# A decode layer with its gradients: key-value moments for dq, half of V kept on chip, 128-row weight layouts, and zero fills on a queue of their own

## Chip, cores and metric

One Trainium2 chip, one core. The time is device microseconds of one launch, from runs without and with the profiler; most agree within 0.3%. The kernel before takes 882.29 us (median of 5 runs, 880.35 to 884.32). All runs in this document are of the undisturbed ("fast") state, except where a single run has no state.

## The reference, cut to what matters

```
x: [1, 1, 448];  k_cache, v_cache: [1, 8, 32768, 256] bf16;  16 query heads, 8 key-value heads
W = 4096                                   # only the last 4096 rows of each cache are used
h   = x + attention(layernorm(x), k_cache[:, :, -W:], v_cache[:, :, -W:], wq, wo)
out = h + (g * u) @ w_down                 # g, u = layernorm(h) @ w_gate, @ w_up
returns out and the gradients of x, k_cache, v_cache, wq, wo, w_gate, w_up, w_down
```

The gradients of the two caches have the caches' shape. Of their 268.4 MB only the last 4096 rows of each head are not zero: 33.5 MB are computed, and 234.9 MB are written as zeros, in 112 fills of 2 MB. Each attention head pair (two query heads share one key-value head) needs K and V of 2.1 MB each.

## The kernel before

It runs in a first pass over the 8 head pairs (scores, softmax, output), a middle (output projection, gated layer, its backward, down to the gradient `do` of the attention output), and a second pass over the head pairs (dp = do V, ds, dq = ds K, and the two cache gradients as outer products). Nearly all transfers, the fills too, stand in one queue, SyncE's.

```python
    LD = nc.sync
    ST = nc.sync
    ...
    def issue_zero_fills(k):
        for _ in range(k):
            if zero_jobs:
                LD.dma_start(out=zero_jobs.pop(0), in_=zeros[:])       # zeros: [128, 8192] bf16
    ...
    wq_sb = wqp.tile([DC, NC, H * Dh], bf16, tag="wq")                  # DC, NC = 112, 4
    ...
    def load_kv_natural(pool, cache, g, tag, nb):
        t_ = pool.tile([128, T, Dh], bf16, tag=tag, bufs=nb)
        LD.dma_start(out=t_[:], in_=cache[0, g, Sk - W:, :].rearrange("(p t) d -> p t d", t=T))
        return t_
    ...
    LD.dma_start(out=wo_sb[:], in_=A_wo.rearrange("(jc p) n -> p jc n", p=128))   # rows of 896 bytes
    ...
    for g in range(G):                                   # first pass
        ...                                              # K^T by TensorE, scores, softmax -> pT_all[:, g]
        for t in range(T):
            nc.tensor.matmul(o_ps[:, :], lhsT=pT16[:, t, :], rhs=V_sb[:, t, :], ...)
        V_tiles[g + 1] = load_kv_natural(kv, A_v_cache, g + 1, "Vnat", 1)
    ...
    for it in range(G):                                  # second pass, g = 7 .. 0
        ...
        issue_zero_fills(Z2_LIST[it])
        if it >= 1 and g - 1 >= 0:
            V2[g - 1] = load_kv_natural(kv, A_v_cache, g - 1, "Vnat", 1)
            K2[g - 1] = load_kv_natural(kv, A_k_cache, g - 1, "Knat", 2)
        ...
        for t in range(T):                               # dq = ds K: K is needed again
            nc.tensor.matmul(dq_ps[:, :], lhsT=dsT16[:, t, :], rhs=K_sb[:, t, :], ...)
```

Of the kernel before, what the change touches and what calls it, by code (L numbers as in the profile page):

```python
# [7 lines left out]
bf16 = mybir.dt.bfloat16  # L8
# [6 lines left out]
DC = 112  # L15
NC = 4
H = 16
# [4 lines left out]
TH = 16  # L22
NR = T // TH
F = 1792
FC = 14
# [5 lines left out]
Z1, ZM, Z2, ZT = 6, 10, 6, 6  # L31
Z2_LIST = [6, 10, 6, 6, 6, 5, 5, 4]
# [3 lines left out]
def kernel(  # L36
        ctx, tc, A_x, A_k_cache, A_v_cache, A_wq, A_wo, B_x, B_w_gate, B_w_up, B_w_down, grad_out,
           out_0, out_1, out_2, out_3, out_4, out_5, out_6, out_7, out_8):
    nc = tc.nc

    const = ctx.enter_context(tc.tile_pool(name="const", bufs=1))
    small = ctx.enter_context(tc.tile_pool(name="small", bufs=2))
    lnp = ctx.enter_context(tc.tile_pool(name="lnp", bufs=1))
    psum_acc = ctx.enter_context(tc.tile_pool(name="psum_acc", bufs=1, space=bass.MemoryType.PSUM))
    psum_tr = ctx.enter_context(tc.tile_pool(name="psum_tr", bufs=2, space=bass.MemoryType.PSUM))
    psum_s = ctx.enter_context(tc.tile_pool(name="psum_s", bufs=1, space=bass.MemoryType.PSUM))
    psum = ctx.enter_context(tc.tile_pool(name="psum", bufs=2, space=bass.MemoryType.PSUM))
    psum_d = ctx.enter_context(tc.tile_pool(name="psum_d", bufs=2, space=bass.MemoryType.PSUM))

    LD = nc.sync  # L50
    ST = nc.sync
# [11 lines left out]
    zeros = const.tile([128, ZW], bf16)  # L63
    nc.vector.memset(zeros[:], 0.0)
    S_f = const.tile([H, 8, 128], f32)
    nc.gpsimd.memset(S_f[:], 0.0)
    nc.gpsimd.affine_select(out=S_f[:], in_=S_f[:], compare_op=ALU.not_equal, fill=1.0, base=0,
                            pattern=[[-1, 8], [1, 128]], channel_multiplier=-8)
    E_b = const.tile([2, 4], bf16)
    nc.gpsimd.memset(E_b[:], 0.0)  # L70
    nc.gpsimd.affine_select(out=E_b[:], in_=E_b[:], compare_op=ALU.not_equal, fill=1.0, base=-2,
                            pattern=[[1, 4]], channel_multiplier=-1)
# [7 lines left out]
    assert len(zero_jobs) == 8 * Z1 + ZM + 8 * Z2 + ZT  # L80

    def issue_zero_fills(k):
        for _ in range(k):
            if zero_jobs:
                LD.dma_start(out=zero_jobs.pop(0), in_=zeros[:])

    tc.swap_default_side()
    wq_pool = tc.tile_pool(name="wq_pool", bufs=1)
    wqp = wq_pool.__enter__()
    wq_sb = wqp.tile([DC, NC, H * Dh], bf16, tag="wq")  # L90
    tc.swap_default_side()
    for k in range(2):
        LD.dma_start(out=wq_sb[:, 2 * k:2 * k + 2, :], in_=A_wq.rearrange("(p c) j -> p c j", c=NC)[:, 2 * k:2 * k + 2, :])
    x_bf = lnp.tile([1, D], bf16, tag="ldrow_bf")
    LD.dma_start(out=x_bf[:], in_=A_x.rearrange("a b d -> (a b) d"))
    x_row = const.tile([1, D], f32)
    nc.vector.tensor_copy(out=x_row[:], in_=x_bf[:])
    go_bf = lnp.tile([1, D], bf16, tag="ldrow_bf")
    LD.dma_start(out=go_bf[:], in_=grad_out.rearrange("a b d -> (a b) d"))
    dh2_row = const.tile([1, D], f32)  # L100
    nc.vector.tensor_copy(out=dh2_row[:], in_=go_bf[:])

    def layernorm_row(xr, tagp):
        stats = lnp.tile([1, nc.vector.BN_STATS_DIM], f32, tag="stats")
        nc.vector.bn_stats(out=stats[:], in_=xr)
        mv = const.tile([1, nc.vector.BN_AGGR_DIM], f32, tag=tagp + "mv")
        nc.vector.bn_aggr(out=mv[:], in_=stats[:])
        rstd = const.tile([1, 1], f32, tag=tagp + "rstd")
        nc.scalar.activation(out=rstd[:], in_=mv[:, 1:2], func=ACT.Sqrt, bias=eps_t[0:1, 0:1], scale=1.0)
        nc.vector.reciprocal(out=rstd[:], in_=rstd[:])  # L110
        xn = const.tile([1, D], f32, tag=tagp + "xn")
        nc.vector.tensor_scalar(out=xn[:], in0=xr, scalar1=mv[:, 0:1], scalar2=rstd[:, 0:1], op0=ALU.subtract, op1=ALU.mult)
        xn_b = const.tile([1, D], bf16, tag=tagp + "xnb")
        nc.vector.tensor_copy(out=xn_b[:], in_=xn[:])
        xT_ps = psum.tile([DC, NC], f32, tag="tmp")
        for c in range(NC):
            nc.tensor.matmul(xT_ps[:, c:c + 1], lhsT=xn_b[0:1, c::NC], rhs=ones_bf[0:1, 0:1], start=True, stop=True)
        xT_b = const.tile([DC, NC], bf16, tag=tagp + "xTb")
        nc.vector.tensor_copy(out=xT_b[:], in_=xT_ps[:])
        xT_f = const.tile([DC, NC], f32, tag=tagp + "xTf")  # L120
        nc.vector.tensor_copy(out=xT_f[:], in_=xT_ps[:])
        return mv, rstd, xn, xn_b, xT_b, xT_f

    def ln_bwd_row(dy_ap, xhat, rstd, tagp):
        dy = lnp.tile([1, D], f32, tag="lnb_dy")
        if len(dy_ap.shape) == 3:
            nc.vector.tensor_copy(out=dy[:].rearrange("o (m c) -> o m c", c=dy_ap.shape[2]), in_=dy_ap)
        else:
            nc.vector.tensor_copy(out=dy[:], in_=dy_ap)
        s1 = lnp.tile([1, 1], f32, tag="lnb_s1")  # L130
        nc.vector.reduce_sum(out=s1[:], in_=dy[:], axis=AX)
        prod = lnp.tile([1, D], f32, tag="lnb_prod")
        s2 = lnp.tile([1, 1], f32, tag="lnb_s2")
        nc.vector.tensor_tensor_reduce(out=prod[:], in0=dy[:], in1=xhat, scale=1.0, scalar=0.0, op0=ALU.mult, op1=ALU.add, accum_out=s2[:])
        m12 = lnp.tile([1, 2], f32, tag="lnb_m12")
        nc.vector.tensor_scalar(out=m12[:, 0:1], in0=s1[:], scalar1=-1.0 / D, scalar2=None, op0=ALU.mult)
        nc.vector.tensor_scalar(out=m12[:, 1:2], in0=s2[:], scalar1=-1.0 / D, scalar2=None, op0=ALU.mult)
        t = lnp.tile([1, D], f32, tag="lnb_t")
        nc.vector.scalar_tensor_tensor(out=t[:], in0=xhat, scalar=m12[:, 1:2], in1=dy[:], op0=ALU.mult, op1=ALU.add)
        dx = lnp.tile([1, D], f32, tag="lnb_dx")  # L140
        nc.vector.tensor_scalar(out=dx[:], in0=t[:], scalar1=m12[:, 0:1], scalar2=rstd[:, 0:1], op0=ALU.add, op1=ALU.mult)
        return dx

    def bcast_row(row_ap, n, dst_bf):
        ps = psum.tile([128, n], f32, tag="tmp")
        nc.tensor.matmul(ps[:], lhsT=ones_f[0:1, 0:128], rhs=row_ap, start=True, stop=True)
        nc.scalar.copy(out=dst_bf, in_=ps[:])  # L147

    evac_ctr = [0]

    def evac_copy(out_ap, in_ap):
        if evac_ctr[0] % 2 == 0:
            nc.scalar.copy(out=out_ap, in_=in_ap)  # L153
        else:
            nc.vector.tensor_copy(out=out_ap, in_=in_ap)  # L155
        evac_ctr[0] += 1

    def load_kv_natural(pool, cache, g, tag, nb):
        t_ = pool.tile([128, T, Dh], bf16, tag=tag, bufs=nb)
        LD.dma_start(out=t_[:], in_=cache[0, g, Sk - W:, :].rearrange("(p t) d -> p t d", t=T))  # L160
        return t_

    def transpose_kv(X_sb, XT, evac=None):
        for q in range(8):
            tr_ps = psum_tr.tile([128, 4, 2, 128], bf16, tag="tr")
            for i in range(4):
                t = 4 * q + i
                for dh in range(2):
                    nc.tensor.transpose(tr_ps[:, i, dh, :], X_sb[:, t, dh * 128:(dh + 1) * 128], ident_bf[:])  # L169
            if evac is None:  # L170
                evac_copy(XT[:, 4 * q:4 * q + 4, :, :], tr_ps[:])
            else:
                evac(out=XT[:, 4 * q:4 * q + 4, :, :], in_=tr_ps[:])

    mv1, rstd1, xn_row, xn_bf, xnT_bf, xnT_f = layernorm_row(x_row[:], "ln1")
    qT_ps = psum.tile([128, 32], f32, tag="tmp")
    for col in range(32):
        for c in range(NC):
            nc.tensor.matmul(qT_ps[:, col:col + 1], lhsT=wq_sb[:, c, col * 128:(col + 1) * 128], rhs=xnT_bf[:, c:c + 1],  # L179
                             start=(c == 0), stop=(c == NC - 1))  # L180
    qT_bf = const.tile([128, 32], bf16)
    nc.vector.tensor_copy(out=qT_bf[:], in_=qT_ps[:])
    wq_pool.__exit__(None, None, None)

    kv_pool = tc.tile_pool(name="kv", bufs=2)
    kv = kv_pool.__enter__()
    work1_pool = tc.tile_pool(name="work1", bufs=2)
    work1 = work1_pool.__enter__()
    K_tiles = [None] * G
    V_tiles = [None] * G  # L190
    K_tiles[0] = load_kv_natural(kv, A_k_cache, 0, "Knat", 2)
    K_tiles[1] = load_kv_natural(kv, A_k_cache, 1, "Knat", 2)
    V_tiles[0] = load_kv_natural(kv, A_v_cache, 0, "Vnat", 1)

    tc.swap_default_side()
# [234 lines left out]
    with tc.tile_pool(name="work2", bufs=2) as work2, tc.tile_pool(name="rows", bufs=1) as rows, \  # L430
            tc.tile_pool(name="dkv", bufs=3) as dkv, tc.tile_pool(name="wgst", bufs=2) as wgst2:
        for it in range(G):
# [8 lines left out]
            for thunk in pending_stores:  # L441
                thunk()
# [140 lines left out]
```

## Time and profile before

| | before |
|---|---|
| time, median of 5 | 882.29 us |
| profiled span | 879.0 us |
| read / written | 76.65 / 280.59 MB |
| DMA queue's share of the 16 DMA engines | 98.8% |
| TensorE / VectorE / ScalarE busy | 47% / 31% / 22% |

The next fence has lines of the profile page of the kernel before. "DMA" is the mean busy share of the 16 DMA engines in 40 equal slices of the span, in tenths (9 is 90% or more); "GB/s" is what they moved.

```profile
span 879.0 us, 8996 instructions
...
PE 415.2 (47%) x3888; PEld 289.1 (33%) x3888; DVE 273.7 (31%) x554; ACT 189.7 (22%) x267; POOL 4.4 (0%) x14
...
DMA  9999999999999999999999999999999999999993
GB/s 289 364 334 428 429 430 426 429 422 431 424 423 428 431 424 426 429 418 429 430 428 430 426 418 429 428 429 429 420 430 429 417 402 424 401 423 354 432 368 122
...
q1 hardware_dynamic: 30180, 357.25, 98.8%
...
HBM read 76.65 MB, written 280.59 MB: 406 GB/s over the span
```

No engine that computes is busy for half of the span, and the DMA engines always are. This kernel is bound by its bytes. The rate is about 428 GB/s in most slices, and less at both ends. The table by stretches shows where. Its columns after the stretch and its length are busy time of TensorE, its weight loads, VectorE, ScalarE and GpSimd (with instruction counts), the granted TensorE clock, the DMA share, and GB/s.

```profile
5.00:10.00 5.00, 0.00 (x0) 0.00 (x0) 0.99 (x3) 0.00 (x0) 0.00 (x0) 1.00 1.00 269
10.00:15.00 5.00, 0.00 (x0) 0.00 (x0) 0.00 (x0) 0.00 (x0) 0.00 (x0) 1.00 0.97 269
...
45.00:50.00 5.00, 3.36 (x62) 2.51 (x59) 1.77 (x6) 0.48 (x4) 0.00 (x0) 1.00 1.04 269
50.00:55.00 5.00, 0.38 (x2) 0.30 (x2) 0.59 (x3) 0.16 (x2) 0.00 (x0) 0.58 1.01 247
...
100.00:200.00 100.00, 40.23 (x501) 31.20 (x500) 13.31 (x36) 14.09 (x24) 0.00 (x0) 0.65 1.01 427
...
800.00:820.00 20.00, 13.96 (x61) 8.91 (x61) 7.51 (x11) 6.28 (x12) 0.00 (x0) 0.53 1.01 365
...
850.00:860.00 10.00, 0.00 (x0) 0.00 (x0) 0.00 (x0) 0.00 (x0) 0.48 (x1) 0.50 0.97 276
860.00:870.00 10.00, 0.00 (x0) 0.00 (x0) 0.00 (x0) 0.00 (x0) 0.00 (x0) 0.50 0.48 161
870.00:879.00 9.00, 0.00 (x0) 0.00 (x0) 0.00 (x0) 0.00 (x0) 0.00 (x0) 0.50 0.09 39
```

From 5 to 15 us the DMA engines are full, yet move 269 GB/s: that is the load of wq in 112 rows. In the packet records of the trace its 16 KB packets take about 975 ns, where 16 KB packets elsewhere take 611 (16 engines times 16 KB in 611 ns are 429 GB/s). The stretch from 45 to 55 us has w_gate and w_up, also in 112 rows, and the first packets of w_down. After 850 us the last stores drain.

### The profile page before, as it was taken

To read this page: it belongs to the slowest core of one execution; us is meant where nothing else is said; L and a number is where in the kernel's file an instruction comes from. 1 tells how busy PE (TensorE), PEld (TensorE's weight loads), DVE (VectorE), ACT (ScalarE), POOL (GpSimd) and SP (SyncE) were. 2 spreads that over 40 slices of the span, in tenths; PEclk is the share of its full clock that TensorE was granted. 3 is DMA by queue.
4 is the path that set the end of the run, shared out by engine and by line. 5 is a ranking of instruction groups with operands and counts; after the bars stand their busy time and mean duration, and the time that the engine had idled before them with its cause. 6 is when DMAs were issued, how large, how long until landed. Compare 5 with 4: busy or idle time off the path is not lost.

```text
span 879.0 us, 8996 instructions
## 1 busy us (share of the span) xinstructions
PE 415.2 (47%) x3888; PEld 289.1 (33%) x3888; DVE 273.7 (31%) x554; ACT 189.7 (22%) x267; POOL 4.4 (0%) x14
## 2 busy tenths in 40 slices
PE   0824425060523208652199486382845748386400
PEld 0813314040413105441164153261623426163300
DVE  3311011020202000357963343432334434334760
ACT  0502011020202004051043132231323324233100
POOL 1000000000000000000000000000000000000000
PEclk9965667575757558655585556575655758575655
DMA  9999999999999999999999999999999999999993
GB/s 289 364 334 428 429 430 426 429 422 431 424 423 428 431 424 426 429 418 429 430 428 430 426 418 429 428 429 429 420 430 429 417 402 424 401 423 354 432 368 122
DMA packets 30283, 357.82 MB, mean 407 GB/s; under 512 B 3010, under 2 KB 7108, under 8 KB 9028
## 3 DMA queue, kind: packets, MB, share of 16 engines
q1 hardware_dynamic: 30180, 357.25, 98.8%
q8 instruction: 30, 0.49, 0.2%
q14 instruction: 9, 0.07, 0.0%
q0 software_dynamic: 64, 0.00, 0.0%
HBM read 76.65 MB, written 280.59 MB: 406 GB/s over the span
## 4 chain that ended last, share of the span: by engine, by line
issue 55%; DMA 31%; PE 8%; SPq 2%; DVE 1%; POOL 0%; ACT 0%; POOLq 0%
PE o_ps L264 5%; DMA t__537<-in_A_v_cache_dram 4%; DMA t__1393<-in_A_v_cache_dram 4%; DMA t__1607<-in_A_v_cache_dram 4%; DMA t__965<-in_A_v_cache_dram 4%; DMA t__1179<-in_A_v_cache_dram 4%; DMA t__751<-in_A_v_cache_dram 4%; DMA t__1819<-in_A_v_cache_dram 3%; DMA wd_sb<-in_B_w_down_dram 2%; DMA x_bf<-in_A_x_dram 2%; SPq L204 2%; PE ao_ps L306 1%; PE ffn_ps L327 1%; PE tr_ps L169 0%; PE qT_ps L179 0%
## 5 line engine op out<-in xcount | busy, mean ns | idle before, releaser
L155 DVE CAST stg<-d_ps 128x512 bf16<-128x512 f32 x128 | 88.2, 689 | 99.4 <-PE d_ps L496 75.5
L153 ACT CAST stg<-d_ps 128x512 bf16<-128x512 f32 x128 | 74.8, 584 | 176.5 <-DMA out_dram<-stg 92.4
L153 ACT COPY KT<-tr_ps 128x1024 bf16<-128x1024 bf16 x32 | 32.3, 1011 | 185.2 <-PE tr_ps L169 185.2
L153 ACT COPY VT<-tr_ps 128x1024 bf16<-128x1024 bf16 x28 | 28.4, 1012 | 54.5 <-PE tr_ps L169 28.6
L155 DVE COPY KT<-tr_ps 128x1024 bf16<-128x1024 bf16 x32 | 22.1, 691 | 47.8 <-PE tr_ps L169 47.7
L155 DVE COPY VT<-tr_ps 128x1024 bf16<-128x1024 bf16 x28 | 19.3, 690 | 31.3 <-PE tr_ps L169 29.7
L496 PE MATMUL d_ps<-R_sb,rows_3486 4*128 4x256 bf16 x64 | 16.2, 375 | 20.4 <-ACT stg L153 17.2
L496 PE MATMUL d_ps<-R_sb,rows_4256 4*128 4x256 bf16 x64 | 16.3, 378 | 19.9 <-ACT stg L153 17.0
L488 PE MATMUL r_ps<-ident_bf,pdsT 128*4 128x128 bf16 x256 | 21.0, 235 | 8.7 <-DVE pdsT L471 3.5
L496 PE MATMUL d_ps<-R_sb,rows_3877 4*128 4x256 bf16 x64 | 16.1, 371 | 18.2 <-ACT stg L153 15.2
L496 PE MATMUL d_ps<-R_sb,rows_3101 4*128 4x256 bf16 x64 | 17.1, 396 | 15.9 <-ACT stg L153 12.7
L496 PE MATMUL d_ps<-R_sb,rows_4633 4*128 4x256 bf16 x64 | 16.3, 377 | 15.2 <-ACT stg L153 12.3
L496 PE MATMUL d_ps<-R_sb,rows_5010 4*128 4x256 bf16 x64 | 15.4, 360 | 15.7 <-ACT stg L153 12.5
L374 DVE CUSTOM_DVE_ANT_0 junk<-wo_sb,dh_bc 128x448 bf16<-128x448 bf16 x32 | 20.0, 625 | 3.6 <-ACT dh_bc L147 2.6
L488 PEld LDWEIGHTS <-pdsT 128*4 128x4 bf16 x256 | 16.5, 90 | 11.9 <-issue 6.9
L286 DVE CAST o_bf<-o_ps 16x256 bf16<-16x256 f32 x1 | 0.4, 413 | 63.3 <-PE o_ps L264 63.3
L351 PE MATMUL bc_ps<-ident_f,dgu_f 128*128 128x128 f32 x56 | 13.1, 413 | 14.1 <-DVE dgu_f L342 10.2
L264 PE MATMUL o_ps<-t__1819,pT_1996 128*16 128x256 bf16 x32 | 5.4, 350 | 29.0 <-DMA t__1819<-in_A_v_cache_dram 29.0
L496 PE MATMUL d_ps<-R_sb,rows_5388 4*128 4x256 bf16 x64 | 15.7, 362 | 7.1 <-ACT stg L153 4.6
L353 ACT CAST dgu_bc<-bc_ps 128x512 bf16<-128x512 f32 (+1 forms) x8 | 15.9, 2296 | 12.8 <-PE bc_ps L351 12.8
L234 PE MATMUL sT_ps<-qT_bf,KT 128*128 128x2 bf16 x512 | 17.6, 164 | 2.0 <-ACT KT L153 2.0
L264 PE MATMUL o_ps<-t__965,pT_1144 128*16 128x256 bf16 x32 | 6.3, 389 | 23.1 <-DMA t__965<-in_A_v_cache_dram 23.1
(271 smaller groups left out, 721.7 us busy)
## 6 DMA issues: line engine op xcount, KB each, us to landing
out_dram<-zeros SPq DMA_DIRECT2D x112, 2048.0 KB, 39.6
out_dram<-stg SPq DMA_DIRECT2D x16, 2048.0 KB, 37.2
out_dram<-sb SPq DMA_DIRECT2D x6, 784.0 KB, 37.1
wq_sb<-in_A_wq_dram SPq DMA_DIRECT2D x2, 1792.0 KB, 12.7
wo_sb<-in_A_wo_dram SPq DMA_DIRECT2D x1, 3584.0 KB, 21.0
out_dram<-sb SPq DMA_DIRECT2D x4, 896.0 KB, 37.2
t__279<-in_A_k_cache_dram SPq DMA_DIRECT2D x1, 2048.0 KB, 19.7
t__281<-in_A_k_cache_dram SPq DMA_DIRECT2D x1, 2048.0 KB, 10.5
```

The source lines that it names most:

```text
L153: nc.scalar.copy(out=out_ap, in_=in_ap)
L155: nc.vector.tensor_copy(out=out_ap, in_=in_ap)
L204: LD.dma_start(out=wg_sb[:, 2 * k:2 * k + 2, :], in_=B_w_gate.rearrange("(p c) f -> p c f", c=NC)[:, 2 * k:2 * k + 2, :])
L234: nc.tensor.matmul(sT_ps[:, t, :], lhsT=KT[:, t, dh, :], rhs=qT_bf[:, 4 * g + dh:4 * g + dh + 3:2], start=(dh == 0), stop=(dh == 1))
L264: nc.tensor.matmul(o_ps[:, :], lhsT=pT16[:, t, :], rhs=V_sb[:, t, :], start=(g == 0 and t == 0), stop=(g == G - 1 and t == T - 1))
L306: nc.tensor.matmul(ao_ps[:], lhsT=oT_bf[:, dh, h:h + 1], rhs=wo_sb[:, jc, :], start=(jc == 0), stop=(jc == 31))
L327: nc.tensor.matmul(ffn_ps[:], lhsT=hhT_bf[:, fc:fc + 1], rhs=wd_sb[:, fc, :], start=(fc == 0), stop=(fc == FC - 1))
L351: nc.tensor.matmul(bc_ps[:, j, :], lhsT=dgu_f[:, i, fc:fc + 1].to_broadcast([128, 128]), rhs=ident_f[:], start=True, stop=True)
L353: nc.scalar.copy(out=dgu_bc[:, i, :].rearrange("p (m fc) -> p fc m", fc=FC)[:, 4 * q:4 * q + nfc, :], in_=bc_ps[:, 0:nfc, :])
L374: nc.vector.tensor_tensor_reduce(out=junk[:], in0=wo_sb[:, jc, :], in1=dh_bc[:], scale=1.0, scalar=0.0, op0=ALU.mult, op1=ALU.add, accum_o ...
L488: nc.tensor.transpose(r_ps[:, i, :], pdsT[:, t, :], ident_bf[:])
L496: nc.tensor.matmul(d_ps[:, i, :], lhsT=rows4[0:4, t * 128:(t + 1) * 128], rhs=R_sb[:, which * Dh:(which + 1) * Dh], start=True, stop=True)
```

## The change

It is a rewrite with three aims.

1. **Fewer bytes.** ds = p (dp - delta) with dp = do V, so dq = sum over keys of ds K = do M - delta kbar, where M = sum of p V K^T (a 256 x 256 matrix for each query head) and kbar = sum of p K. Both are summed in the first pass, while K and V are on chip, and the second pass does not need K. The V tiles of the last four head pairs stay on chip. Loads of K and V fall from 29 to 20.
2. **128-row layouts.** Of the 448 rows of wq, w_gate and w_up 384 go to 128 partitions with three rows each, and the other 64 are cut into halves on 128 partitions. w_down and wo are cut differently too; a partition's share of wo is one run of 28 KB.
3. **Fills on a queue of their own.** All 112 zero fills are issued from GpSimd at the start of the program, beside SyncE's queue with the loads and stores.

Its price is arithmetic: 64 moment matmuls of 512 columns and 64 scalings of K on VectorE for each head pair. The diff, cut to its core:

```diff
-    def issue_zero_fills(k):
-        for _ in range(k):
-            if zero_jobs:
-                LD.dma_start(out=zero_jobs.pop(0), in_=zeros[:])
+    for job in zero_jobs:
+        ZQ.dma_start(out=job, in_=zeros)                 # ZQ = nc.gpsimd
 ...
-    wq_sb = wqp.tile([DC, NC, H * Dh], bf16, tag="wq")   # 112 rows
+    wq_A = A_wq[0:384, :].rearrange("(p c) j -> p c j", c=3)
+    wq_B = A_wq[384:D, :].rearrange("r (h j) -> (r h) j", h=2)
+    LD.dma_start(out=wqA, in_=wq_A)
+    LD.dma_start(out=wqB, in_=wq_B)
 ...
+        def moments(g, p_f):                             # first pass
+            for c in range(8):
+                for i in range(4):
+                    for hh in range(2):
+                        nc.vector.tensor_scalar(out=pK[:, i, hh, :], in0=K_sb[:, t, :], scalar1=p_f[:, t, hh:hh + 1], ...)
+                for i in range(4):
+                    for vh in range(2):
+                        nc.tensor.matmul(M_ps[:, vh, :], lhsT=V_sb[:, t, vh * 128:(vh + 1) * 128], rhs=pK[:, i, :, :]..., ...)
+            for k, X_sb in enumerate((V_sb, K_sb)):      # output and kbar
+                for dh in range(2):
+                    for t in range(T):
+                        nc.tensor.matmul(ok_ps[:, k, dh, :], lhsT=X_sb[:, t, dh * 128:(dh + 1) * 128], rhs=pT_all[:, g, t, :], ...)
 ...
-                LD.dma_start(out=wo_sb[:], in_=A_wo.rearrange("(jc p) n -> p jc n", p=128))
+                LD.dma_start(out=wo_sb, in_=A_wo.rearrange("(p j) n -> p j n", j=32))
 ...
+    # second pass: dq from M and kbar, before any head pair
+    nc.tensor.matmul(dqb_ps[...], lhsT=doT_f[:, vh, h:h + 1].to_broadcast([128, 128]), rhs=M_sb[g][:, vh, hh, :], ...)
+    nc.tensor.matmul(dqb_ps[...], lhsT=ndk[:, kh, h:h + 1].to_broadcast([128, 128]), rhs=ident_f[:], ...)
-            for t in range(T):
-                nc.tensor.matmul(dq_ps[:, :], lhsT=dsT16[:, t, :], rhs=K_sb[:, t, :], ...)
+            if it < 2:                                   # V of four head pairs alone is loaded again
+                load_kv(V_slot[it], A_v_cache, order[HELD + it])
+            elif it in (HELD, HELD + 1):
+                load_kv(V_slot[it % 2], A_v_cache, order[it + 2])
```

The rest of the diff rearranges the buffers into one large one (three K slots and four V slots instead of two and one), computes the small rows in 128 columns, and forms the cache gradients with 32-row matmuls of 512 columns.

## The prediction

> **What bounds the kernel now.** Bytes. The page's queue table: one hardware queue holds the 16 DMA engines 98.8% of the 879.0 us span and moves 357.25 MB. PE is busy 47%, DVE 31%. In the table by stretches the rate is flat at 425 to 431 GB/s from 60 to 700 us. Below that: 269 GB/s at 5-15 us (wq load, 112 rows), 247-341 at 30-55 us (weights in 112 rows, wo in 896-byte rows), 410 at 700-800, 365 at 800-820, and 276, 161 and 39 in the last 30 us, where the queue waits 28.6 us for the final 112-row dwq stores. At 429 GB/s the bytes would need 833 us; about 46 us is lost to slow layouts and the tail.
>
> **What the change does.**
> 1. Removes the second pass over K (6 reloads) and part of that over V (7 reloads become 4). K and V loads: 29 before, 8 + 8 + 4 = 20 after; 9 x 2.097 = 18.9 MB less. Total about 338.5 MB; at 429 GB/s minus 44 us, all on the critical resource.
> 2. 128-row layouts for all weights: most of the other losses go.
> 3. Zero fills (112 x 2.097 = 234.9 MB) go out from GpSimd, from the first microseconds, and absorb any gap in the load/store queue. [...] so I expect no extra bandwidth, only no gaps.
>
> **Is compute still hidden?** It grows. Estimates from this trace's durations, per head pair:
> - First pass, PE: 64 transposes (~0.065 us in the chain) 4.3; 64 score matmuls (~0.06) 3.8; 64 moment matmuls of 512 columns (twice 0.17, the 256-column output matmul) 22; 128 two-column matmuls 7.7: about 38 us at the mean clock of 0.63, perhaps 26 if denser work raises it. DVE: 64 scalings at 0.2-0.27, 13-17 us. So 210 to 300 us for eight.
> - Middle: about 100 us.
> - Second pass: 32 evacuations of 128x512 (0.689 DVE, 0.584 ACT), VT copies, about 50 us of weight gradients in all: about 220 us.
>
> Sum about 530-640 us. The non-fill bytes, 104 MB, need 484 us at a half share (~214 GB/s). Fills then still remain, so they finish last, near the byte limit; compute stays off the critical path.
>
> **Predicted:** 338.5 MB / 429 GB/s = 789, plus about 11 for start and tail, plus about 4 between trace span and timed run: **804 us**, 8 in 10 between 791 and 838. Faster by over 2%: 0.91; within 2%: 0.04; slower: 0.05.
>
> **What would show it.** Right: about 338 MB; two queues with big shares; 425-430 GB/s from the first to the last slice; compute's last piece long before the end; the last chain a zero fill; PE clock above 0.63 in the first pass. Wrong steps: total rate under 415 GB/s (the software queue costs bandwidth); fills ending early and a compute- or store-bound tail well under 400 GB/s (unfair shares starve the loads, or the compute chain is over ~700 us).
>
> **What would make it wrong.** Fills taking far more than half of the engines; [...] false dependencies between slices of the one big buffer, serialising loads behind fills.

Two passages are cut above, where marked: a clause on how two queues share the engines, and one of the dangers. That no extra bandwidth was expected agrees with the queue table, with the engines held for 98.8% of the span by one queue. The half share behind the 484 us is the author's assumption, half of the measured 429 GB/s; no trace had then shown how two queues share.

## The result, and the profile after

The changed kernel takes **819.87 us** (median of 5 runs, 819.06 to 824.67), against 882.29 before. The ratio is 0.9301 (95% interval 0.9275 to 0.9328). Here and below, a ratio is the mean time of one kernel's fast runs over the mean of the other's in the same rounds, so it is not quite the ratio of the medians. Each group of experiments below ran beside the kernel before on its own chip; that one's medians were 881.89, 882.86 and 882.20 us. The changed kernel itself was not timed again, so experiments on it are compared through the kernel before.

| | before | after |
|---|---|---|
| time, median | 882.29 us | 819.87 us |
| profiled span | 879.0 us | 822.9 us |
| read / written | 76.65 / 280.59 MB | 57.89 / 280.59 MB |
| TensorE / VectorE busy | 47% / 31% | 47% / 43% |

The page of the changed kernel; q0 is GpSimd's queue, with the fills, and q1 SyncE's.

```profile
span 822.9 us, 10750 instructions
...
PE 385.7 (47%) x4365; PEld 248.4 (30%) x4365; DVE 356.1 (43%) x1116; ACT 193.7 (24%) x301; POOL 62.1 (8%) x120
...
DMA  8999999999999999999999999999999999999991
GB/s 333 429 431 428 428 427 427 429 429 428 426 428 419 424 431 431 426 422 424 405 429 426 407 428 427 422 431 404 427 432 425 428 423 426 422 426 422 421 390 45
...
q0 software_dynamic: 16128, 234.89, 67.6%
q1 hardware_dynamic: 8774, 103.60, 30.0%
...
HBM read 57.89 MB, written 280.59 MB: 411 GB/s over the span
```

The 57.89 MB read are exactly the count of tiles in the prediction. The rate is now high from the second slice on. The table by stretches of the changed kernel:

```profile
0.00:5.00 5.00, 0.00 (x0) 0.00 (x0) 3.33 (x1) 1.28 (x1) 1.08 (x8) 1.00 0.52 117
5.00:10.00 5.00, 1.60 (x11) 1.10 (x11) 3.87 (x24) 0.29 (x1) 4.34 (x8) 1.00 0.97 354
...
200.00:250.00 50.00, 49.94 (x612) 29.08 (x610) 34.71 (x167) 15.18 (x25) 4.62 (x9) 0.97 1.01 427
...
350.00:400.00 50.00, 28.86 (x268) 26.20 (x267) 17.90 (x50) 10.12 (x15) 4.25 (x8) 0.75 1.01 416
...
650.00:700.00 50.00, 8.27 (x52) 1.72 (x51) 16.94 (x27) 14.22 (x27) 3.48 (x7) 0.50 1.01 426
700.00:750.00 50.00, 1.23 (x8) 0.22 (x8) 3.17 (x5) 2.57 (x5) 4.25 (x8) 0.50 1.00 422
750.00:775.00 25.00, 0.00 (x0) 0.00 (x0) 0.00 (x0) 0.00 (x0) 2.66 (x5) 0.50 1.00 421
...
800.00:810.00 10.00, 0.00 (x0) 0.00 (x0) 0.00 (x0) 0.00 (x0) 0.00 (x0) 0.50 0.29 126
810.00:815.00 5.00, 0.00 (x0) 0.00 (x0) 0.00 (x0) 0.00 (x0) 0.00 (x0) 0.50 0.06 26
815.00:823.00 8.00, 0.00 (x0) 0.00 (x0) 0.00 (x0) 0.00 (x0) 0.00 (x0) 0.50 0.01 6
```

TensorE and VectorE are done a little after 700 us; nothing computes in the last 100 us. The clock in the dense part of the first pass is 0.97, against 0.65 and less in most of the kernel before. So the work that was added is hidden. The waits of the changed kernel (who waited for whom: total us, times, longest) say the same:

```profile
POOL out_dram L111 <- DMA out_dram<-arena: 712.7, 104, 12.9
...
ACT arena L556 <- DMA out_dram<-arena: 75.6, 7, 16.5
...
DVE arena L559 <- DMA out_dram<-arena: 60.6, 6, 15.0
```

GpSimd waited for earlier fills and nothing else of weight: it issued eight fills without a wait, and each of the other 104 as soon as one of the eight in flight had landed (104 waits, 712.7 us). ScalarE and VectorE waited for stores in the second pass, because a staging buffer came free only when its store had landed (75.6 us and 60.6 us above).

Three numbers from these lines give the time. 339.17 MB at 429 GB/s are 790.6 us. The first 10 us move 2.36 MB, 5.5 us worth, so 4.5 us are lost. From 800 us on 1.4 MB are moved in 23 us, so 19.6 us are lost. Between, the mean rate is 424.5 GB/s rather than 429, which is 8.2 us. Together 822.9.

The tail is the largest loss, and the trace says what it is made of. In the semaphore events each fill has 16 completions (1792 for the 112 fills), and the page counts 16 DMA engines. These are the times of the 16 completions of the last transfer to land, read from the semaphore events of the traces (us):

```
before     last store:                    first 855.3  median 864.7  second last 875.4  last 877.7
after      last fill:                     first 796.1  median 802.1  second last 810.6  last 817.5
```

From 745 us on the packet records of the changed kernel fall into 16 chains, in which each packet starts as the one before it ends: as many as DMA engines, and each chain ends 0.3 to 0.4 us before one of the 16 completions. All have nearly the same mean time for a packet (618 to 624 ns), but one engine still has 117 of the 16 KB packets to do, the others 81 to 105. So the engines are not unequally fast at the end; some are behind. The kernel waits for the one that is furthest behind.

### The profile page after: what moved, and what is told of

Read it like the earlier page. It is cut to its first block, busy times and chain, and to the rows that moved or that the text cites. A ratio compares the mean times of both kernels' runs of the same rounds, so it can differ in the third digit from the quotient of the medians.

```text
span 822.9 us, 10750 instructions
## 1 busy us (share of the span) xinstructions
PE 385.7 (47%) x4365; PEld 248.4 (30%) x4365; DVE 356.1 (43%) x1116; ACT 193.7 (24%) x301; POOL 62.1 (8%) x120
## 2 busy tenths in 40 slices
DMA packets 24951, 339.17 MB, mean 412 GB/s; under 512 B 2755, under 2 KB 3398, under 8 KB 4422
## 3 DMA queue, kind: packets, MB, share of 16 engines
HBM read 57.89 MB, written 280.59 MB: 411 GB/s over the span
## 4 chain that ended last, share of the span: by engine, by line
another core or an unknown queue 54%; DMA 33%; POOL 4%; issue 3%; DVE 0%; POOLq 0%
DMA out_dram<-arena 33%; POOL out_dram L111 4%; DVE arena L83 0%; POOLq L608 0%
## 5 line engine op out<-in xcount | busy, mean ns | idle before, releaser
L267 DVE TENSOR_SCALAR arena<-arena,p_f 128x256 bf16<-128x256 bf16 x512 | 114.6, 282 | 54.5 <-PE M_ps L271 53.7
L271 PE MATMUL M_ps<-arena 128*128 128x512 bf16 x512 | 132.2, 396 | 8.1 <-DVE arena L267 8.0
L551 PE MATMUL d_ps<-arena,rT 32*128 32x512 bf16 x256 | 46.9, 583 | 154.1 <-ACT arena L556 81.1
L111 POOL DMA_DIRECT2D out_dram<-arena x112 | 61.0, 545 | 716.5 <-DMA out_dram<-arena 712.7
L228 ACT COPY arena<-tr_ps 128x1024 bf16<-128x1024 bf16 x64 | 62.3, 1014 | 83.6 <-PE tr_ps L227 82.6
L559 DVE CAST arena<-d_ps 128x512 bf16<-128x512 f32 x64 | 43.6, 682 | 60.6 <-DMA out_dram<-arena 60.6
L505 PE MATMUL tr_ps<-ident_bf,arena 128*128 128x128 bf16 x512 | 61.1, 289 | 15.6 <-ACT arena L507 8.6
L271 PEld LDWEIGHTS <-arena 128*128 128x128 bf16 x512 | 48.5, 102 | 52.5 <-issue 11.3
L507 ACT COPY arena<-tr_ps 128x1024 bf16<-128x1024 bf16 x32 | 32.5, 1015 | 112.9 <-PE tr_ps L505 65.1
L555 ACT CAST arena<-d_ps 128x512 bf16<-128x512 f32 x64 | 37.5, 586 | 80.6 <-PE d_ps L551 80.5
L227 PE MATMUL tr_ps<-ident_bf,arena 128*128 128x128 bf16 x512 | 47.3, 251 | 19.6 <-DMA arena<-in_A_k_cache_dram 19.6
L558 DVE CAST arena<-d_ps 128x512 bf16<-128x512 f32 x64 | 44.1, 689 | 27.2 <-PE d_ps L551 27.0
L556 ACT CAST arena<-d_ps 128x512 bf16<-128x512 f32 x64 | 38.0, 593 | 75.6 <-DMA out_dram<-arena 75.6
L505 PEld LDWEIGHTS <-arena 128*128 128x128 bf16 x512 | 46.6, 131 | 22.0 <-issue 15.7
L227 PEld LDWEIGHTS <-arena 128*128 128x128 bf16 x512 | 37.0, 113 | 20.8 <-DMA arena<-in_A_k_cache_dram 20.1
L512 PEld LDWEIGHTS <-arena 128*128 128x128 bf16 x512 | 19.9, 107 | 45.5 <-DVE arena L509 37.7
L277 PEld LDWEIGHTS <-arena 128*128 128x128 bf16 x1024 | 28.0, 97 | 3.3 <-issue 1.7
L277 PE MATMUL ok_ps<-pT_all,arena 128*128 128x2 bf16 x1024 | 27.8, 164 | 0.0
L231 PEld LDWEIGHTS <-arena 128*128 128x128 bf16 x512 | 19.8, 99 | 19.4 <-ACT arena L228 14.1
```

The source lines that it names most:

```text
L111: ZQ.dma_start(out=job, in_=zeros)
L227: nc.tensor.transpose(tr_ps[:, i, dh, :], K_sb[:, 4 * q + i, dh * 128:(dh + 1) * 128], ident_bf[:])
L228: nc.scalar.copy(out=KT, in_=tr_ps[:])
L267: nc.vector.tensor_scalar(out=pK[:, i, hh, :], in0=K_sb[:, t, :], scalar1=p_f[:, t, hh:hh + 1], scalar2=None, op0=ALU.mult)
L271: nc.tensor.matmul(M_ps[:, vh, :], lhsT=V_sb[:, t, vh * 128:(vh + 1) * 128], rhs=pK[:, i, :, :].rearrange("p h d -> p (h d)"), start=(t == ...
L277: nc.tensor.matmul(ok_ps[:, k, dh, :], lhsT=X_sb[:, t, dh * 128:(dh + 1) * 128], rhs=pT_all[:, g, t, :], start=(t == 0), stop=(t == T - 1))
```

## The experiments

Theory A, formed from the profile after: the gain is bytes and layouts; the time is the work of the busiest DMA engine; and that engine is busiest because it fetches TensorE's instructions beside its share of the data. The changed kernel's trace has 34 packets of 16 KB in the queue q8, which the page lists as one of instructions, of 0.88 to 1.02 us each. Its 4365 matmuls and as many weight loads are 257 for each such packet; in the kernel before, 3888 of each and 30 packets, 259. The expectations below count one fetch for about so many TensorE instructions: an estimate from these two traces. That the packets of q8 are TensorE's is no more than this count until the next two runs. Rival B: the software queue makes one engine slow, or the tail has another cause. Rival C: compute is on the critical path after all.

### TensorE instructions added

```diff
+            dm_ps = ps_t.tile([128, 2], f32, tag="tmp", name="dm_ps")
+            for i in range(256):                          # for each of the 8 head pairs of the second pass
+                nc.tensor.matmul(dm_ps[:], lhsT=(ident_bf if i % 2 else ones_bf)[:], rhs=ident_bf[:, 0:2], start=True, stop=True)
             for o_ap, st_ in ((out_3, stV), (out_2, stK)):
```

> The changed kernel with 2048 extra tiny matmuls (256 per head pair of the second pass), results unchanged: about 4096 more TensorE instructions, 16 more 16 KB instruction fetches (34 to about 50), 0.26 MB more. Theory A (all TensorE instruction fetches run on one DMA engine, which falls behind the other 15 by 0.6 to 0.95 us for each, and the kernel ends when that engine has done its share of the fills): the spread of the last fill's 16 completions grows from 21 us by 10 to 15 us, and the time by as much, 820 to 830-835 us. Rival B (the software queue makes one DMA engine slow, or the tail comes from something else): spread and time as before within 2 us.

Measured: 831.62 us (830.46 to 833.27), ratio to the kernel before 0.9422 (0.9403 to 0.9442), against 0.9301 of the changed kernel: 1.2% of 882 us, about 11 us more. The trace has 50 instruction packets in q8: 16 more for about 4096 more TensorE instructions, and none but TensorE's were added. The last fill:

```
after      34 fetches   first 796.1  median 802.1  second last 810.6  last 817.5
pe_more    50 fetches   first 796.0  median 801.3  second last 809.5  last 826.1
```

Fifteen engines ended where they ended without the extra instructions. One ended 8.6 us later, 0.54 us for each of 16 fetches, a little less than the 611 ns that a 16 KB data packet takes. The extra matmuls did not make the compute chain end last: TensorE's last work begins before 709 us here and before 703 us in the changed kernel. Theory A holds as far as completions show it: the delay of the added fetches fell to one of 16.

### TensorE instructions taken away

```diff
-                    for t in range(T):                    # output and kbar sums
+                    for t in (0, T - 1):
                         nc.tensor.matmul(ok_ps[:, k, dh, :], ...)
-                    for dh in range(2):                   # scores, and likewise dp
+                    for dh in range(1):
                         nc.tensor.matmul(sT_ps[:, 4 * q + i, :], ...)
-                for i in range(4):                        # moment matmuls: half of them
+                for i in ((0, 1, 2) if c == 0 else (1, 2, 3) if c == 7 else (1, 2)):
```

> The changed kernel with TensorE work left out (wrong on purpose: of the 128 output and key-sum matmuls of a head pair 8 are kept, half of the score, dp and moment matmuls): about 3400 fewer TensorE instructions, 13 fetches fewer. Theory A: the last fill's spread shrinks from 21 us to 9-14 us and the time falls by 7 to 12 us, to 808-813 us. Rival B: no change in the tail; the time stays at 818-821 us, since compute is not on the critical path. Rival C (compute is on the critical path after all): the time falls by more than 12 us and the total DMA rate in the middle rises.

Measured (a wrong result): 814.60 us (813.45 to 817.93), ratio 0.9240 (0.9215 to 0.9265), about 5 us less; 21 fetches. The last fill's completions: first 795.2, median 799.7, second last 806.3, last 806.8. The spread is 11.6 us, within the expectation; the time fell a little less than expected. The fetching engine is 10.7 us earlier and no longer stands out: another engine, at 806.3, is as late. That is the floor that taking away fetches can reach, and why the engines other than the fetching one differ by some 10 us was not found. The sizes read from completions are rough, as each is from one profiled execution: in other runs below that also have 34 fetches the last engine comes 1.7 us (engine_probe), 2.6 (fills_more) and 8.2 (rows112) after the next one. The finding rests on the times, which do not overlap: 813.45 to 817.93 us with 21 fetches, 819.06 to 824.67 with 34, 830.46 to 833.27 with 50. Rival C falls: over a fifth of TensorE's busy time was taken away (385.7 to 299.1 us on the page), and the time moved by no more than the tail did.

### Nine fills more

```diff
-    for job in zero_jobs:
+    for job in zero_jobs + zero_jobs[:9]:
         ZQ.dma_start(out=job, in_=zeros)
```

> The changed kernel with the first nine zero fills written a second time at the end of their queue, results unchanged: 18.87 MB more, which is what the change took away. If the DMA engines' bytes alone set the time: plus 18.87 MB / 429 GB/s = 44 us, 862-865 us. If part of the time is something else that the extra fills could hide under: less than 35 us more.

Measured: 861.92 us (860.22 to 865.63), ratio 0.9776 (0.9748 to 0.9804): the ratio is 0.0475 above the changed kernel's 0.9301, and 0.0475 of 882 us are 42 us for 18.87 MB, 2.2 us for each MB. At 429 GB/s they would be 44 us, so bytes set the time at the full rate. Two thirds of the gain of 62 us are the bytes that the change does not move.

### Only the queue, in the kernel before

```diff
-                LD.dma_start(out=zero_jobs.pop(0), in_=zeros[:])
+                nc.gpsimd.dma_start(out=zero_jobs.pop(0), in_=zeros[:])
 ...
+    issue_zero_fills(len(zero_jobs))                      # all 112, at the start
```

> The kernel before with one part of the change alone: its 112 zero fills go out from GpSimd, all at the start of the program, bytes as before (357.25 MB). Theory: at 429 GB/s 833 us, plus a start of about 5 and a tail of 15-25 us of lagging engines: 850-870 us, against 882; so the queue of its own is worth 15 to 30 us, and the saved bytes the rest (about 44). Rival: the fills already filled every gap, so their own queue is worth nothing (878-886 us), and the whole gain is bytes and layouts.

Measured: 1024.49 us (1021.50 to 1026.38), ratio 1.1610 (1.1579 to 1.1641): 142 us slower than the kernel before. Neither expectation came near. The trace shows two causes. First, its timeline of GpSimd:

```profile
447.79 0.53 POOL L85 DMA_DIRECT2D out_dram<-zeros  x1 [4.32 <-DMA out_dram<-zeros]
821.59 0.50 POOL L550 DMA_DIRECT2D out_dram<-dx_bf  x1 [373.27 <-DVE dx_bf L549]
822.09 3.71 POOL L85 DMA_DIRECT2D out_dram<-zeros  x7
```

The small store of the dx row stood in GpSimd's queue ahead of the last fills and waited for its data for 373 us: an artefact of this edit, mended in the next run. Second, the stretches and the issue of wo (the last column is us from issue to landing):

```profile
100.00:200.00 100.00, 0.00 (x0) 0.00 (x0) 0.00 (x0) 0.00 (x0) 10.13 (x19) 0.50 1.01 428
```

```profile
wo_sb<-in_A_wo_dram SPq DMA_DIRECT2D x1, 3584.0 KB, 171.4
```

TensorE did nothing at all from 100 to 200 us, at 428 GB/s. The load of wo took 171.4 us; in the kernel before it is 21.0:

```profile
wo_sb<-in_A_wo_dram SPq DMA_DIRECT2D x1, 3584.0 KB, 21.0
```

From 60 to 200 us the packet records hold 3743 packets of 896 bytes and 3416 of 16 KB. Nearly one to one, but equal bundles of rows would give that too, so the order matters: followed from 60 to 150 us, each of the 16 chains has one row of wo, one row of a fill, one row of wo, and so on (two rows of wo in about one turn of eight, which is where a packet of 4 bytes of the fills' queue comes in between; the changed kernel's trace has 16 of these for the 128 rows of a fill, one for every eight). So in this run the engines took turns between the two queues, and a turn was one row: the queue with 896-byte rows got 896 bytes for about every 16 KB of its neighbour.

### The same, with the small rows sent from SyncE

```diff
-        STP = nc.gpsimd
+        STP = nc.sync
```

> As before_own_queue, but the two small result rows leave from SyncE, so that the fill queue is not held up from 448 to 822 us by the dx row that stood in it. That hold-up was an artefact of the first try and should be gone: no gap in the fills. The 171 us of the wo load, whose 896-byte rows took turns with 16 KB fill rows, stays. Expected 880-930 us, TensorE idle from 100 to 200 us as before. If the hold-up alone had made the first try slow: about 860 us.

Measured: 909.72 us (907.76 to 911.32), ratio 1.0306 (1.0285 to 1.0327), as expected. The hold-up is gone and wo still takes 171.4 us. So the separate queue, put alone into the kernel before, costs 27 us.

### The fills held back until wo has landed

```diff
+    hold = const.tile([128, 2], bf16)
+    nc.gpsimd.tensor_copy(out=hold[:], in_=wo_sb[:, 31, 446:448])
+    issue_zero_fills(len(zero_jobs))
```

> As before_own_queue2, but GpSimd starts the fills only when wo has landed (a tiny copy of two of its elements stands ahead of them). Theory (queues take turns row by row, so a load in small rows starves beside fills in large rows): the wo load lands in about 20-25 us instead of 171, TensorE is not idle from 100 to 200 us, and the time is 30 us or more below before_own_queue2, about 850-880 us. Rival (the fills starve every load, whatever its rows): the first pass still stands still, and the time stays within 15 us of before_own_queue2.

Measured: 911.34 us (905.12 to 917.48), ratio 1.0325 (1.0271 to 1.0379). The mechanism was right and the time was not. The first pass no longer stands still, and wo lands in 46.4 us:

```profile
100.00:200.00 100.00, 59.00 (x684) 48.91 (x685) 17.62 (x48) 19.28 (x33) 5.84 (x11) 0.72 1.01 427
...
600.00:700.00 100.00, 47.51 (x354) 28.99 (x351) 29.17 (x47) 24.86 (x37) 4.64 (x8) 0.58 1.01 401
700.00:800.00 100.00, 46.70 (x344) 31.98 (x344) 47.53 (x56) 19.68 (x30) 6.74 (x10) 0.60 0.98 385
800.00:915.00 115.00, 0.00 (x0) 0.00 (x0) 0.00 (x0) 0.00 (x0) 6.91 (x13) 0.50 0.63 261
```

```profile
wo_sb<-in_A_wo_dram SPq DMA_DIRECT2D x1, 3584.0 KB, 46.4
```

But the time won there was lost again at the end: compute ends before 800 us and the fills end at 910. In the last fill 14 of the 16 completions come by 881.4 us, one at 888.9 and one at 910.3. The last engine is 31 us behind the median, further than in any other run, and the rate from 600 to 800 us is also low. From 800 to 850 us, with fills alone left, the DMA engines are busy for a share of 0.82 only, at 334 GB/s, and GpSimd, which has eight fills in flight, waits up to 15.1 us for one to land, where it waits 4.3 us from 837 us on. This fits engines that ran dry while all waited for the one behind. Why that one fell so far behind in this run was not tested; this stays open. What is shown is that in the kernel before the queue of its own brings no gain with or without the starved load.

### wo in short rows, in the changed kernel

```diff
-                LD.dma_start(out=wo_sb, in_=A_wo.rearrange("(p j) n -> p j n", j=32))
+                for a in range(2):
+                    LD.dma_start(out=wo_sb[:, a::2, :], in_=A_wo.rearrange("(p j) n -> p j n", j=32)[:, a::2, :])
```

> The changed kernel, with wo loaded to the same places in 896-byte rows (two transfers of every second row) instead of 28 KB runs; results unchanged. Theory of turns row by row: the load takes 130-180 us instead of about 20, the middle starts that much later (the first gate matmul at 390-440 us instead of 280), the fills run ahead meanwhile and end first, and the time rises to 860-900 us with a tail well under 400 GB/s. Rival (shares are by bytes): at half share the load takes about 20 us and the time stays at 818-824.

Measured: 833.94 us (828.99 to 836.18), ratio 0.9430 (0.9394 to 0.9466). Stretches, and the two transfers of wo:

```profile
300.00:350.00 50.00, 0.53 (x1) 0.08 (x1) 0.00 (x0) 0.00 (x0) 5.33 (x10) 0.50 1.01 428
...
750.00:835.00 85.00, 15.63 (x101) 3.59 (x98) 35.73 (x66) 26.98 (x50) 0.00 (x0) 0.50 0.61 260
```

```profile
arena<-in_A_wo_dram SPq DMA_DIRECT2D x2, 1792.0 KB, 80.3
```

The two halves take 80.3 us each, one after the other, 160 us, and TensorE stands idle from 272 to 350 us and nearly so to 400. In the changed kernel the 128 packets of 28 KB that bring wo stand in the packet records from 245.7 to 261.1 us, 15.4 us beside the same fills. The theory of turns row by row holds, and the 28 KB runs of wo are a condition of the separate queue in this kernel, not an extra. The time rose less than expected. Everything after wo came about 120 us later, and 11 us (by the ratios) to 14 us (by the medians) of that reached the end. The changed kernel has about 100 us between the end of its compute and its own end, and the delay used that up first: now the last 85 us run at 260 GB/s, with the fills gone, and compute and its own stores left. This is the measure of how much slack the compute chain has.

### Which engine fetches? A probe

```diff
+        for k in range(1, 16):
+            LD.dma_start(out=zero_jobs[k - 1][0:k, 0:256 * (k + 1)], in_=zeros[0:k, 0:256 * (k + 1)])
```

> The changed kernel with 15 tiny stores at the end of the load/store queue, of 1 to 15 rows, each with its own row size (1 to 8 KB), zeros onto zeros; results unchanged, time unchanged within 3 us. [...]

A sentence is cut above.

Measured: 821.94 us, a single run of unknown state. The stores of k rows did make k packets each. But they were issued not at the end, as they depend on nothing there, but between 93 and 176 us, where both queues are busy, and many packets start within a few ns of each other. I followed the chains of packets and placed the fetching engine among five that I called 9 to 13, names that rest on assumption. The next experiment shows that this reading was wrong; the probe settles nothing.

### Work moved between the DMA engines

```diff
-    for job in zero_jobs:
+    for job in zero_jobs[:-1]:                            # balance2: [:-2]
         ZQ.dma_start(out=job, in_=zeros)
+    for job in zero_jobs[-1:]:                            # balance2: [-2:]
+        LD.dma_start(out=job.rearrange("(e r) f -> e r f", e=8), in_=zeros[0:32:4].unsqueeze(1).to_broadcast([8, 16, ZW]))
```

> The changed kernel with one of its 112 fills cut into 8 rows of 16 x 16 KB instead of 128 rows of 16 KB, in the load/store queue: by the probe it then runs on DMA engines 0 to 7 alone, and the engine that fetches TensorE's instructions (9 to 13 by the probe) has 8 packets less, 4.9 us. Theory A: the last completion of the last fill comes 2 to 5 us earlier, and the time falls by as much, to 815-818 us. If that engine is among 0 to 7: it rises by about 5 us. If the tail has another cause: no change.

> The same with two fills: engines 0 to 7 have 16 packets more, the others 16 less. Theory A: the fetching engine ends 10 us earlier, but now the busiest of engines 0 to 7 may end last; time 3 us either side of balance1, spread of the last fill well under 21 us.

"Engines 0 to 7" are the name for the eight on which, by that reading of the probe, an 8-row transfer runs. That it runs on eight is seen only in the result below, in two groups of eight completions; no trace shows an engine's number.

Measured: 827.46 us (824.28 to 829.40), ratio 0.9371 (0.9349 to 0.9392) with one fill moved, and 829.41 us (828.21 to 835.12), ratio 0.9411 (0.9384 to 0.9438) with two. Both slower than 0.9301. The completions of the last fill:

```
after      796.1 796.9 799.4 799.7 800.1 800.6 800.6 801.9 802.3 802.6 803.0 804.1 807.6 809.9 810.6 817.5
balance1   791.2 794.0 794.3 794.3 794.7 795.0 795.7 795.8 | 806.7 806.7 806.8 807.5 812.6 813.7 816.2 822.3
balance2   797.4 797.4 797.5 797.5 797.5 797.5 797.6 797.9 | 806.6 806.8 806.9 807.1 812.1 812.2 813.2 828.0
```

With one fill moved the engines fall into two groups of eight, 10.9 us apart, close to the 16 packets of 611 ns (9.8 us) by which their loads now differ. The last engine is in the late group, 4.8 us later than it was, 8 packets; with two fills moved 10.5 us later, 16 packets being 9.8. So the fetching engine is one of the eight that an 8-row transfer uses. That is the case named beforehand ("if that engine is among 0 to 7"), and the opposite of what the probe had said. It confirms the main point: in these runs what one DMA engine has to do sets the end of the kernel. The distance of the two groups does not grow with the second fill, though 32 packets are 19.6 us: the early eight end within 0.5 us of each other, and from 600 to 650 us the DMA share is 0.95, at 404 GB/s, where the changed kernel has 1.01 and 428. So engines that were ahead had probably stood idle; this was not followed further. The mend in the right direction, taking packets from those eight, was not made.

### 112-row transfers, brought back for K and V

```diff
-        LD.dma_start(out=dst, in_=cache[0, g, Sk - W:, :].rearrange("(p t) d -> p t d", t=T))
+        src = cache[0, g, Sk - W:, :].rearrange("(p t) d -> p t d", t=T)
+        LD.dma_start(out=dst[0:112], in_=src[0:112])
+        LD.dma_start(out=dst[112:128], in_=src[112:128])
```

> The changed kernel with each of its 20 K and V loads cut into rows 0 to 111 and rows 112 to 127; bytes, data and results unchanged. Before the change a 16 KB packet of a 112-row load took about 990 ns where a 128-row one takes 611. If 112 rows cost that here too: 20 x 112 packets x 0.38 us / 16 engines = 53 us more DMA time, and the time rises by 30 to 55 us, to 850-875 us. If it costs only where several such packets run side by side, and the fills between them hide it: less than 10 us, below 830 us.

Measured: 832.44 us (831.60 to 832.94), ratio 0.9432 (0.9417 to 0.9447): about 12 us more. Between the two expectations: 112 rows cost engine time, but a quarter of what the wq load at the start of the kernel before would have suggested. A 16 KB packet between 60 and 250 us takes 641 ns on average here, 615 in the changed kernel, and about 975 in that wq load (the 990 of the expectation is the mean of its first 10 us), where nearly all packets were such, at a DMA share of 0.97 to 1.00, and no fills lay between.

### The fills back in one queue, in the changed kernel

```diff
-    for job in zero_jobs:
-        ZQ.dma_start(out=job, in_=zeros)
+    def fills(k):
+        for _ in range(min(k, len(zero_jobs))):
+            LD.dma_start(out=zero_jobs.pop(0), in_=zeros)
 ...                          # fills(3) after the first loads, fills(4) after each head pair of the first pass,
 ...                          # fills(27) after the gate weights, fills(6) ahead of each head pair of the second, the rest last
```

> The changed kernel with its fills put back into the load/store queue of SyncE, in portions among the other transfers (3 at the start, 4 per head pair of the first pass, 27 in the middle, 6 per head pair of the second, the rest at the end); results and bytes unchanged (338.5 MB). If the queue of its own is what keeps the engines full in this kernel: gaps where the one queue waits for stores or buffers, rate below 415 GB/s in places, 835-870 us. If one queue can do as well (as it did before the change): 815-826 us.

Measured: **813.86 us** (813.68 to 814.49), ratio 0.9224 (0.9209 to 0.9238), results correct. The interval does not overlap that of the changed kernel (0.9275 to 0.9328). This is the fastest correct kernel; the separate queue costs about 6 us rather than gaining anything. The page:

```profile
span 812.2 us, 10771 instructions
...
GB/s 349 426 423 427 428 428 430 427 430 426 425 429 420 427 429 432 430 428 431 426 432 418 415 431 427 428 429 431 430 408 430 434 427 431 426 427 430 432 432 116
...
q1 hardware_dynamic: 24902, 338.49, 98.3%
```

There are no gaps for a second queue to fill: after the first slice one slice is below 415 GB/s before the end (408). Sixteen completions of its last transfer: first 793.6, median 797.8, second last 800.4, last 811.3. Two things are better than in the changed kernel. The 16 KB packets take 614.6 ns on average instead of 618.5, which is 19,000 x 3.9 ns / 16 = 4.6 us (616.7 to 618.8 ns in the other runs with a separate queue, rows112 apart, so 2.5 to 5 us); after 740 us, when the changed kernel has fills from GpSimd alone in flight, its packets take 620.7 ns against 611.2 here. And the first fifteen engines end within 6.8 us instead of 14.5. One engine still ends 10.9 us after all others, with all fills and loads in SyncE's queue: so the late engine is not made by the software queue, and this part of rival B falls. Why packets of the software queue take longer is not shown.

## Why the prediction was right, and where it was not

The time was inside the range (791 to 838) and 16 us above the middle, 804.

- **Bytes: right.** 338.5 MB were predicted; the page has 57.89 + 280.59 = 338.48. Nine fills put back cost 42 us, where 44 were expected. This is the main part of the gain.
- **Layouts: right in sign and about in size.** The packet records, summed over the engines and divided by 16, give 870.8 us of engine time before, of which 36.7 are beyond 611 ns for 16 KB; and 805.8 and 15 us after. So bytes took 43.5 us off and faster packets 21.5. I had about 46 us of slow layouts and tail, and expected most of it to go. The packets' part did; the tail's did not. This split is a sum over packet records: no run changed the weights' layouts alone, so their share of the measured time is argued and not shown.
- **A queue of its own: wrong.** The step was that the fills "absorb any gap in the load/store queue", and that this is worth the removal of gaps. One queue had none to remove in this kernel: one_queue is faster by 6 us. In the kernel before, the separate queue alone makes it 27 us slower. That no bandwidth was to be had from a second queue was right: no stretch of 5 us or more that was read of the changed kernel is above 433 GB/s, and the kernel before, with one queue, has 436 from 25 to 30 us.
- **Compute hidden: right, with one stage too short.** First pass: 210 to 300 us predicted, about 230 in the trace (32 to 262 us). Middle: 100, about 140 in the trace. Second pass: 220, about 300, since its staging buffers wait for stores (75.6 us of ScalarE's and 60.6 us of VectorE's waits above) that share the engines with the fills. wo_small shows that about 100 us of delay in this chain cost nothing. The clock in the first pass is 0.87 from 42 to 272 us (0.65 in the kernel before from 100 to 200), as foreseen.
- **Start and tail: the term that was mis-sized.** "About 11 for start and tail" measured 4.5 + 19.6 = 24 us, and the rate between is 424.5 rather than 429 GB/s, another 8 us. The plus of 4 for the timed run was a minus of 3: the profiled run is the slowest of the five. The end of the tail is one DMA engine, which by these runs also fetches TensorE's instructions: shown by adding (last engine 8.6 us later) and taking away (10.7 us earlier), and by moving its data packets. In the profiled run it accounts for the last 6.9 us; the 14.5 us over which the other fifteen end are not explained.
- **What I named as dangers.** Fills taking far more than half: it happened where the loads' rows are short, in the kernel before with the fills in their own queue (wo in 171.4 us, not 21.0) and in wo_small (160 us), and the changed kernel escapes it by its long runs. The prediction tied this danger to no row length and gave no reason why it would not come, so that wo's long runs were part of the same change was luck for this step. A second danger, of VectorE against the fills: no trace had shown it, and none does: GpSimd's waits are for landed fills (712.7 us), and the rate is 428 GB/s from 300 to 350 us, where VectorE is at its busiest (39.3 of 50 us). False dependencies in the one big buffer: none seen, as loads run beside the fills from the start.

## What to carry to other kernels

Where the profile shows the DMA engines full from end to end, count the bytes first: each MB saved here was worth 2.2 us, and arithmetic added to save them was free as long as its chain ended before the transfers. In these runs a second queue added no bandwidth (813.86 us without it, 819.87 with it), took turns row by row with the first, and starved what stood in short rows beside long ones (896 bytes beside 16 KB: 171.4 us for a load of 21.0); move transfers there only if the trace shows gaps. When all transfers end together except for a tail, look at the completions of the last one engine by engine: here one engine ended 6.9 us after the others, and 8.6 us later still when 16 instruction fetches were added.
